# An attention kernel on one core: the order of the 64-query and 192-query pieces in the middle score fill

## The chip, the cores and the metric

The kernel runs on one NeuronCore of a Trainium2 chip. The metric is device time in microseconds (us), the median of the runs that are quoted. The kernel before takes 819.46 us (3 runs, 819.17 to 820.69).

## The reference

```python
B, H, Sq, Sk, D = 16, 32, 192, 1024, 128          # q, k, v are bf16, small random numbers
def reference(q, k, v):
    scale = q.shape[-1] ** -0.5
    scores = jnp.einsum("bhqd,bhkd->bhqk", q, k) * scale
    p = _softmax(scores, axis=-1)
    return jnp.einsum("bhqk,bhkd->bhqd", p, v)
```

There are 512 heads. For each of them the scores are 192 x 1024, softmax runs over the 1024 keys, and the result is 192 x 128.

## The kernel before

The kernel works on **quads** of four heads, 128 of them. Scores are computed transposed, with keys on the partitions: eight tiles of 128 keys times 192 queries give 1536 columns per head. These are made in three **thirds** of 512 columns (one PSUM bank per head). For each third PE (TensorE) runs a **fill** (the score matmuls), ACT (ScalarE) takes the exponential out of PSUM in two instructions, and PE then runs one **PV pass** (32 matmuls) for data of four thirds earlier. So PE's stream is fill, PV, fill, PV, and so on.

In a fill each head has its own 32 rows of the PE array, and the 128-long dot product is done in four passes `w` of 32. Four matmuls, one per head, that differ only in the row group make a **set** below. How a third's 512 columns are cut into pieces is in `CUTS`, as (key tile, first query, last query):

```python
CUTS = (
    (((0, 0, 192),), ((1, 0, 192),), ((2, 0, 128),)),
    (((3, 0, 192), (2, 128, 192)), ((4, 0, 192), (5, 0, 64))),
    (((5, 64, 192),), ((6, 0, 192),), ((7, 0, 192),)),
)
```

The first third has three groups of one piece (12 sets: 192 eight times, 128 four times), the last third the same with the 128 first. The middle third has two groups of two pieces, which alternate: 192, 64, 192, 64, ..., 16 sets. In the code below, shortened and with comments added, a semaphore `s_x` is the one that the trace calls `f_x`.

```python
def take(s, c):
    pe.wait_ge(s, c).then_inc(s, -c)        # wait until s >= c, then take c off it

def qk(f):                                  # fill f: quad x, third b
    x, b = divmod(f, 3)
    if b == 0:
        take(s_qt, 1)
    take(s_kt, 1)
    take(s_e1, 1)
    for group in CUTS[b]:
        for w in range(4):
            h, c = divmod(w, 2)
            for g, (t, n0, n1) in enumerate(group):
                c0 = t * SQ + n0 - 512 * b
                for a in range(4):
                    ...                     # S = the bank of head a, r = its 32 rows
                    ins = pe.matmul(S[:, c0: c0 + n1 - n0],
                                    kt[r, x % NKT, 2 * t + h, :, c],
                                    qt[r, x % R, h, n0:n1, c],
                                    start=w == 0 and g == 0, stop=w == 3, ...)
    ins.then_inc(s_qk, 1)

def pv(s, part=(0, 32)):                    # PV pass s, called after fill s + 4
    x, i = divmod(s, 3)
    if part[0] == 0:
        if i == 0:                          # stands after a MIDDLE fill
            take(s_e3, 3)                   # three exps of the quad are done
            take(s_vp, 2)                   # V is laid out
        if s == NF - 4:
            pe.wait_ge(s_e3, 2)
        elif s < NF - 4 or s == NF - 1:
            take(s_on, 1)                   # the output bank has been read
    ...                                     # 32 matmuls of 129 columns
```

DVE (VectorE) turns each K load and also normalises each PV result, in one order, so a late K holds back a normalisation; PE's next PV pass waits for that one (`f_on` in the trace, `s_on` in the code). And the loads go out on one queue in the order V, K, q, with two additional waits at the start:

```python
for n in range(2, NKN):
    if n == 2:
        e.wait_ge(s_qk, PRE + 1)            # hold V of quad 0
    load_v(n - 2)
    if n == 2:
        e.wait_ge(s_pv, BLANK - 2)          # hold K of quad 2
    load_k(n)
    load_q(e, n)
```

## Time and profile before

| | value | view |
|---|---|---|
| span | 816.9 us | page, head |
| PE busy | 99% | page, part 1 |
| ACT busy | 92% | page, part 1 |
| DMA | 9 tenths or more in 38 of 40 slices, about 405 GB/s | page, part 2 |
| DVE waits for a K load | 15.3 us, 11 times | waits |
| one quad on PE | 2058 + 2107 + 2048 = 6213 ns | matmul starts in the trace |

The head of the page and the rows of part 2 (each digit is the busy share of one fortieth of the span, in tenths):

```profile
span 816.9 us, 71709 instructions
PE 806.7 (99%) x32996; PEld 717.5 (88%) x32996; DVE 599.7 (73%) x1293; ACT 749.8 (92%) x772; POOL 550.7 (67%) x648
...
PE   8999999999999999999999999999999999999997
...
DMA  7999999999999999999999999999999999999992
```

PE and DMA are both full nearly all the time.

The timeline of the kernel before, PE only, for a little over one quad (start us, length us, engine, line, what, count; starts of the next line give the beat, since matmuls overlap):

```profile
397.32 1.10 PE L646 MATMUL f_s<-f_qt,f_kt 32*128 32x192 bf16 x48
398.35 1.10 PE L673 MATMUL f_o<-f_vp,f_pt 128*64 128x129 bf16 x32
399.38 1.10 PE L646 MATMUL f_s<-f_qt,f_kt 32*128 32x192 bf16 x64
400.45 1.10 PE L673 MATMUL f_o<-f_vp,f_pt 128*64 128x129 bf16 x32
401.49 1.09 PE L646 MATMUL f_s<-f_qt,f_kt 32*128 32x128 bf16 x48
402.50 1.10 PE L673 MATMUL f_o<-f_vp,f_pt 128*64 128x129 bf16 x32
403.53 0.35 PE L646 MATMUL f_s<-f_qt,f_kt 32*128 32x192 bf16 x8
```

The fills take 1.03, 1.07 and 1.01 us from their start to the start of their PV pass. The middle one (x64) is the longest although all three stream the same number of columns: that is what the change goes for.

### The profile page before, as it was taken

Reading aid. Unit: us, or ns where it says so; the run is one execution under the profiler, and the core shown is the slowest. Engines: PE = TensorE matmul, PEld = TensorE weight load, DVE = VectorE, ACT = ScalarE, POOL = GpSimd, SP = SyncE. Lnnn points to the kernel's source line nnn. Section 1 sums busy time; section 2 is a strip of 40 time slices with the busy share of each in tenths; the row PEclk is TensorE's granted clock in tenths of the full one; section 3 lists DMA queues with packets and bytes.
Section 4 is the critical chain, followed back from the end, with each engine's and each line's share of the span. In section 5 each row is a group of like instructions: output and inputs, shape, how many; then the busy total and the mean of one; then the engine's idle time right before and its main releaser. Section 6 shows DMA issues by size and latency. Waiting matters only on the chain. (4 is left out here: it accounts for less than half of the span.)

```text
span 816.9 us, 71709 instructions
## 1 busy us (share of the span) xinstructions
PE 806.7 (99%) x32996; PEld 717.5 (88%) x32996; DVE 599.7 (73%) x1293; ACT 749.8 (92%) x772; POOL 550.7 (67%) x648
## 2 busy tenths in 40 slices
PE   8999999999999999999999999999999999999997
PEld 6888888888888888888888888888888888888886
DVE  4777777777777777777777777777777777777775
ACT  6899999999999999999999999999999999999995
POOL 5667766766776676677667666766766676676664
PEclk9999999999999999999999999999999999999999
DMA  7999999999999999999999999999999999999992
GB/s 269 401 402 405 410 403 406 408 403 406 409 401 407 408 403 409 408 402 409 407 403 408 407 403 407 405 405 400 397 406 403 382 411 397 389 404 387 402 368 70
DMA packets 138294, 319.16 MB, mean 391 GB/s; under 512 B 7184, under 2 KB 56336, under 8 KB 121872
## 3 DMA queue, kind: packets, MB, share of 16 engines
q1 hardware_dynamic: 105376, 294.22, 91.9%
q10 hardware_dynamic: 32880, 24.58, 9.0%
q14 instruction: 32, 0.26, 0.1%
q8 instruction: 6, 0.10, 0.0%
HBM read 293.60 MB, written 25.17 MB: 390 GB/s over the span
## 5 line engine op out<-in xcount | busy, mean ns | idle before, releaser
L831 ACT ACTIVATE f_pt<-f_s 128x1536 bf16<-128x1536 f32 x384 | 554.9, 1445 | 0.0
L601 POOL COPY f_kt<-f_kx 128x768 uint32<-128x768 uint32 (+1 forms) x384 | 301.0, 784 | 254.2 <-DVE f_kx L736 254.1
L673 PE MATMUL f_o<-f_vp,f_pt 128*64 128x129 bf16 x12368 | 425.8, 222 | 2.9 <-PEq L629 1.9
L646 PE MATMUL f_s<-f_qt,f_kt 32*128 32x192 bf16 (+1 forms) x20528 | 423.2, 226 | 2.4 <-PEq L629 1.8
L673 PEld LDWEIGHTS f_o<-f_vp,f_pt 128*64 128x64 bf16 x12368 | 366.1, 110 | 55.2 <-issue 28.1
L646 PEld LDWEIGHTS f_s<-f_qt,f_kt 32*128 32x128 bf16 x20528 | 348.5, 92 | 38.9 <-issue 3.1
L736 DVE STREAM_TRANSPOSE f_kx<-f_kn 128x768 uint32<-128x768 uint32 (+1 forms) x384 | 334.0, 870 | 15.7 <-DMA f_kn<-in_k_dram 15.3
L828 ACT ACTIVATE f_pt<-f_s 128x512 bf16<-128x512 f32 x384 | 229.3, 597 | 58.7 <-PE f_s L646 25.6
L610 POOL COPY f_vp<-f_vs 128x1024 uint32<-128x1024 uint32 x256 | 259.9, 1045 | 1.8 <-DMA f_vs<-in_v_dram 1.8
L757 DVE RECIPROCAL f_rinv<-f_o 128x2 f32<-128x2 f32 x381 | 64.9, 170 | 183.2 <-PE f_o L673 183.0
L761 DVE TENSOR_TENSOR f_ob<-f_o,f_rinv 128x256 bf16<-128x256 f32 x381 | 161.7, 424 | 13.3 <-DVE f_rinv L757 0.3
L745 DVE STREAM_TRANSPOSE f_qt<-f_qn 128x384 uint32<-128x384 uint32 x128 | 73.1, 571 | 0.0
L814 ACT ACTIVATE f_pt<-f_ones 128x1536 f32<-128x1536 bf16 x3 | 4.2, 1472 | 0.0
L589 POOL MEMSET f_vp<- 128x1088 uint32 (+1 forms) x3 | 3.8, 1309 | 0.0
L673 PE MATMUL f_s<-f_vp,f_pt 128*64 128x129 bf16 x96 | 3.1, 220 | 0.2 <-PEq L629 0.2
L673 PEld LDWEIGHTS f_s<-f_vp,f_pt 128*64 128x64 bf16 x96 | 2.9, 110 | 0.3 <-issue 0.3
L814 ACT ACT_TABLE_LOAD x1 | 1.3, 1283 | 1.2 <-PEq L859 1.2
L686 PE MATMUL f_o<-f_ones 128*128 128x512 bf16 x2 | 1.0, 622 | 1.1 <-POOL f_ones L586 1.1
L710 DVE MEMSET f_pt<- 128x256 uint32 x4 | 1.1, 272 | 0.9 <-PEq L859 0.9
L703 PE MATMUL f_o<-f_bad,f_ones 128*1 128x1 bf16 x1 | 0.2, 164 | 1.3 <-DVEq L803 1.3
L757 DVE RECIPROCAL f_rinv<-f_s 128x2 f32<-128x2 f32 x3 | 0.5, 170 | 1.2 <-PE f_s L673 1.2
L703 PEld LDWEIGHTS f_o<-f_bad,f_ones 128*1 128x1 bf16 x1 | 0.1, 79 | 1.4 <-DVEq L803 1.4
(15 smaller groups left out, 6.5 us busy)
## 6 DMA issues: line engine op xcount, KB each, us to landing
f_kn<-in_k_dram SPq DMA_DIRECT2D x128, 1024.0 KB, 18.1
f_vs<-in_v_dram SPq DMA_DIRECT2D x128, 1024.0 KB, 16.3
f_qn<-in_q_dram SPq DMA_DIRECT2D x127, 192.0 KB, 14.2
out_dram<-f_ob ACTq DMA_DIRECT2D x62, 384.0 KB, 9.5
out_dram<-f_ob SPq DMA_DIRECT2D x1, 384.0 KB, 3.1
out_dram<-f_ob SPq DMA_DIRECT2D x2, 192.0 KB, 2.0
f_qn<-in_q_dram ACTq DMA_DIRECT2D x1, 192.0 KB, 5.2
```

What stands on the lines that cost most here:

```text
L589: return gp.memset(part.bitcast(U32), 0x3F803F80)
L601: gp.tensor_copy(kt[:, x % NKT].bitcast(U32).rearrange("p U (j s u) c -> p U j s (u c)", s=2, u=2)[:, lo:hi], kx[:, x % 2].rearrange("p (U ...
L610: gp.tensor_copy(vp[:, x % NVP, 2 * T * i: 2 * T * i + 2 * T, 0:D].bitcast(U32), vs[:, x % NVS, 2 * i: 2 * i + 2, :].rearrange("p a (t d) ...
L646: ins = pe.matmul(S[:, c0: c0 + n1 - n0], kt[r, x % NKT, 2 * t + h, :, c], qt[r, x % R, h, n0:n1, c], start=w == 0 and g == 0, stop=w == 3 ...
L673: ins = pe.matmul(O[64 * z: 64 * z + 64, u, 0:129], pt[:, x % R, 2 * y + z, t * SQ + 64 * j: t * SQ + 64 * j + 64], vp[:, x % NVP, (2 * y ...
L736: dve.transpose(kx[:, x % 2].rearrange("p (U s j u) -> p s u U j", s=2, j=32, u=2)[:, :, :, lo:hi], kn[:, x % NKN].rearrange("p (s u U i) ...
L745: dve.transpose(qt[:, x % R].bitcast(U32).rearrange("p b (y j u) c -> p u y b (j c)", y=3, u=2), qn[:, x % NKN].rearrange("p (u y b i) -> ...
L757: dve.reciprocal(ri, O[:, :, 128]).then_inc(s_rc, 1)
L761: dve.tensor_tensor(ob[:, so, 6 * a + 2 * w: 6 * a + 2 * w + 2, :], O[:, :, 0:128], ri.unsqueeze(2).to_broadcast([128, 2, D]), ALU.mult,). ...
L814: return act.activation(part.bitcast(F32), ones[:, 0:1].to_broadcast([128, 2 * T * SQ // 2]), ACT_FN.Copy)
L828: act.activation(pt[:, x % R, 0, c], s1_ps[:], ACT_FN.Exp, scale=scale).then_inc(s_e1, 1)
L831: act.activation(pt[:, x % R, 1:4, c], s3_ps[f % 2][:], ACT_FN.Exp, scale=scale).then_inc(s_e3, 1)
```

## The change: intent and diff

The idea: a fill that ends on a 64-query matmul gives PE little streaming under which to load the weights of the PV pass that follows. With the 64-query piece first, the fill ends on a 192-query matmul. Nothing is added or removed.

```diff
 CUTS = (
     (((0, 0, 192),), ((1, 0, 192),), ((2, 0, 128),)),
-    (((3, 0, 192), (2, 128, 192)), ((4, 0, 192), (5, 0, 64))),
+    (((2, 128, 192), (3, 0, 192)), ((5, 0, 64), (4, 0, 192))),
     (((5, 64, 192),), ((6, 0, 192),), ((7, 0, 192),)),
 )
```

## The prediction

> **What bounds the kernel now.** On the profile page PE is busy 99% of an 816.9 us span: 128 quads (four heads), each three fills and three PV passes. From the last PV matmul before a fill to the last one after it, the trace's matmul starts give medians of 2058 ns (first third), 2107 (middle), 2048 (last): 6.213 us per quad. Between 25 and 801 us no step is over 30 ns off its median, so PE paces that stretch. ACT does not: in the timeline each first exp starts about 50 ns after its fill has ended.
>
> DMA is as close. The page's DMA row reads 9 in nearly every slice, at about 405 GB/s. By packet durations one engine's share of a quad is 8 K packets of 309 ns, 32 V packets of 84, 8 q packets of 65, 16 store packets of 36: about 6.28 us (estimate). The landing records show the 16 engines drifting apart: a K load's first and last arrivals are 1.3 us apart near 55 us, 9 us near 750 us. The last engine decides; its K landings come 6.21 us apart up to quad 76 and 6.26 us after. From K's landing to its use by DVE it is 1 to 2 us in mid-run, 0.02 us by quad 124. DMA has nothing to spare. The Trainium skill, "DMA: Bandwidth & Descriptors" (Latency and other measured facts), says engines 7 and 15 are usually slower; the trace agrees that some lag, but does not number them.
>
> **What the change does.** Nothing is added or removed; only PE's order differs: in the middle fill the sets (four matmuls, one per row group) go 64,192,... instead of 192,64,....
>
> - Close: from the last fill matmul's start to the first PV matmul's it is 160 ns after a 64, 143 after a 128, 172 after a 192. Less streaming (27, 53, 80 ns, estimates from set pitches) 133, 90 and 92 ns are exposed: about 40 ns of PV's weight load is not hidden behind the short matmul. The Trainium skill, "TensorE: Matmul & The Clock Gate" (Part 2), says the next weights load while a matmul runs; these numbers agree.
> - Open: the second set follows the first by 98 ns after 192, 70 after 128: pitch plus 12 to 18 ns. After a 64 I expect 45 to 60 ns, so at most 15 is given back.
>
> Net on PE: middle 2107 -> about 2065 ns (25 to 50 saved), 128 times: 3 to 6.5 us, all on PE's path.
>
> **What remains.** PE would want a quad every 6.17 us; the slowest DMA engine delivers one every 6.21 to 6.26. K's slack is used up earlier, then DVE waits for K, and normalisation and PE behind it. The last K landing (796.15 us) hardly moves; the end can gain about 1 us of slack between DVE and PE. The unprofiled times (819.17 to 820.69; 818.63 profiled) suggest that some runs already wait for DMA.
>
> **Prediction:** 818.9 us, 80% range 816.3 to 820.4. Chances: faster by over 2% 0.005, within 2% 0.985, slower by over 2% 0.01.
>
> **What would show it.** (1) Middle period down 25 to 50 ns, other thirds unchanged. (2) Last fill matmul to first PV matmul in the middle: about 172 ns. (3) In the waits, DVE for the K load grows from 15.3 us to 18 or more, and PE steps well over their median appear from mid-run. (4) Last K landing within 1.5 us of 796.
>
> **What would make it wrong.** If the slow engine speeds up when buffers come free sooner, the whole PE saving shows: 813 to 816 us. If opening on 64 exposes a full weight load (over 40 ns), PE gains nothing.

## The result

| | time, us | runs |
|---|---|---|
| before | 819.32 median (818.6 to 820.69) | 4 |
| changed | 819.79 median (818.35 to 820.86) | 4 |

The ratio is 1.0003, with a 95% interval of 0.9982 to 1.0023: the same. (Ratios here are the mean time of one kernel's fast runs over that of the other's fast runs of the same rounds, so they are not quite the ratio of the medians.) The time lies in the predicted range. The trace, however, does not look as predicted. The head of the changed kernel's page:

```profile
span 817.9 us, 71709 instructions
PE 807.0 (99%) x32996; PEld 718.0 (88%) x32996; DVE 599.3 (73%) x1293; ACT 749.9 (92%) x772; POOL 550.7 (67%) x648
...
DMA  7999999999999999999999999999999999999992
```

PE's timeline of the changed kernel, one quad:

```profile
398.44 1.09 PE L646 MATMUL f_s<-f_qt,f_kt 32*128 32x192 bf16 x48
399.46 1.10 PE L673 MATMUL f_o<-f_vp,f_pt 128*64 128x129 bf16 x32
400.49 1.09 PE L646 MATMUL f_s<-f_qt,f_kt 32*128 32x64 bf16 x64
401.57 1.10 PE L673 MATMUL f_o<-f_vp,f_pt 128*64 128x129 bf16 x32
402.60 1.09 PE L646 MATMUL f_s<-f_qt,f_kt 32*128 32x128 bf16 x48
```

The middle fill begins with 64-column matmuls now, but the PV pass after it still comes 1.08 us after the fill's start (401.57 less 400.49). And in the waits, the line for the K load (us in total, times, longest) reads, before and changed:

```profile
DVE f_kx L736 <- DMA f_kn<-in_k_dram: 15.3, 11, 6.3
DVE f_kx L736 <- DMA f_kn<-in_k_dram: 14.0, 6, 6.9
```

The wait has not grown. So the saving was not made on PE and then hidden by DMA. It was not made on PE at all.

The start times of single records tell where it went. The trace also records PE's semaphore waits: each `take` is a record of the sequencer of 51 ns, whose start is taken here as the moment when it went through (where PE really waits, it comes 37 to 40 ns after the end of what it waits for). For one middle fill of the kernel before, asked by the line of `take`, the view shows three of them:

```profile
L629 PEldq EVENT_SEMAPHORE  x3: 51/51/51, 400.0 to 400.3; - x3
```

Medians over the middle fills, in ns after the start of the last PV matmul before the fill:

| | before | changed |
|---|---|---|
| first matmul of the fill | 153 | 152 |
| second set | 252 | 192 |
| last matmul of the fill | 1069 | 1007 |
| `f_e3` taken | 815 | 816 |
| `f_vp` taken | 971 | 972 |
| `f_on` taken | 1122 | 1123 |
| first PV matmul | 1229 | 1230 |
| last PV matmul (the period) | 2107 | 2107 |

The reordering did what it was meant to: the last matmul of the fill starts 62 ns earlier, and the opening on a 64 gives little back. (The 62 ns are not all gain: in a fill, one set of 192 follows the next after 85 ns and one of 64 after 29, so the last matmul streams some 56 ns longer.) But the first PV matmul starts at the same nanosecond, and so do the three takes ahead of it, one every 150 ns. Each was satisfied well before PE's sequencer came to it: in the kernel before, what they wait for had ended at -871 ns (ACT's exp), 522 ns (POOL's copy of V) and 892 ns (DVE's normalisation). In the other two thirds there is only the take of `f_on`, 40 ns after DVE is done. The sequencer is late because of what it does before: it takes `f_e1` ahead of the fill at -123 ns, 37 ns after ACT's exp has ended, and comes to `f_e3` 939 ns later, with the 64 matmuls of the fill in between (935 ns in the changed kernel). This is read from the traces; no run varies it.

### The profile page after: what moved, and what is told of

Same layout as the page of the kernel before. It is cut to its first block, busy times and chain, and to the rows that moved or that the text cites. A ratio compares the mean times of both kernels' runs of the same rounds, so it can differ in the third digit from the quotient of the medians.

```text
span 817.9 us, 71709 instructions
## 1 busy us (share of the span) xinstructions
PE 807.0 (99%) x32996; PEld 718.0 (88%) x32996; DVE 599.3 (73%) x1293; ACT 749.9 (92%) x772; POOL 550.7 (67%) x648
## 6 DMA issues: line engine op xcount, KB each, us to landing
f_kn<-in_k_dram SPq DMA_DIRECT2D x128, 1024.0 KB, 18.1
```

## The experiments

**Theory T:** the three takes in a row, some 150 ns each on PE's sequencer, hold the PV pass after the middle fill at the same moment in both orders. **Rival W:** the array itself holds it (PV's weight load, a drain), as the prediction had read it. A second question is the prediction's other half: **would DMA have hidden a saving** if there were one?

### e1 and e2: one of the three waits moved ahead of the fill

The exps that `s_e3` counts have ended long before the middle fill starts, and the fill's own wait for `s_e1` implies them (ACT works in order), so the take can stand there without a stall (in e1 `f_e1` is still taken 38 ns after ACT's exp has ended). e1 is this on the changed kernel, e2 on the kernel before.

```diff
 def qk(f):
     ...
     take(s_kt, 1)
+    if b == 1:
+        take(s_e3, 3)
     take(s_e1, 1)
 ...
 def pv(s, part=(0, 32)):
         if i == 0:
-            take(s_e3, 3)
+            if s >= NF - LAG:
+                take(s_e3, 3)
             take(s_vp, 2)
```

> The changed kernel, with PE's wait for the third exp count (f_e3) of the PV pass after the middle fill moved ahead of that fill, between its waits for f_kt and f_e1; it is implied there by f_e1, so it costs no stall. Theory T (three semaphore waits in a row, about 150 ns each on PE's sequencer, hold the first PV matmul after the middle fill at the same moment in both orders): the last of the waits comes about 150 ns earlier, the first PV matmul comes at about 1030 to 1080 ns instead of 1230 after the last PV matmul before the fill, limited by the fill itself; middle period 2107 -> 2050 to 2065 ns early in the run. Rival W (PE is held by something in the array, such as the weight load of PV or a drain): period stays within 10 ns of 2107. For the time: if DMA leaves no room, 818 to 820 us with waits for K by DVE growing; if DMA has room, about 813 us.

> The kernel before with the same move of the wait. Theory T: the middle fill ends on a 64 and the first PV matmul can then follow the last fill matmul by about 115 to 120 ns instead of 160 (streaming 27 plus the 90 that the other fills show); middle period about 2060 to 2070 ns, so the order of the pieces is worth at most about 10 ns once the wait is gone. Rival (the prediction's reading, that 133 ns after a 64 is an exposed weight load): gap stays near 160, period near 2107, and e1 is some 50 ns per middle fill better than e2.

PE's timeline of e1, one quad:

```profile
199.38 1.09 PE L648 MATMUL f_s<-f_qt,f_kt 32*128 32x64 bf16 x64
200.41 1.10 PE L676 MATMUL f_o<-f_vp,f_pt 128*64 128x129 bf16 x32
201.44 1.09 PE L648 MATMUL f_s<-f_qt,f_kt 32*128 32x128 bf16 x48
```

The PV pass now comes 1.03 us after the middle fill's start, not 1.08. In medians, in ns after the last PV matmul before the fill:

| | before | changed | e2 (before + move) | e1 (changed + move) |
|---|---|---|---|---|
| last matmul of the fill | 1069 | 1007 | 1069 | 1007 |
| `f_on` taken | 1122 | 1123 | 970 | 973 |
| first PV matmul | 1229 | 1230 | 1185 | 1177 |
| period of the middle third | 2107 | 2107 | 2063 | 2054 |
| last fill matmul to first PV matmul | 160 | 223 | 116 | 170 |

Theory T holds and W falls. Moving one wait, with no change to any matmul, takes 44 ns off the old order and 53 ns off the new one. It is not the whole 150 ns, since the fill itself then sets the moment; the expectation of e1 had the first PV matmul at 1030 to 1080 ns, too early, but the period in its range. And the gap after a 64 is 116 ns in e2: the old order had no badly hidden weight load either. Take the streaming off (estimated by the pitch of the sets within a fill: medians of 29, 57 and 85 ns for 64, 128 and 192 columns; the prediction's 27, 53 and 80 are a little under them) and 116, 143 and 170 ns leave 87, 86 and 85 ns: what PE needs from a fill to a PV pass is the same whatever the fill ends on. The Trainium skill, "TensorEngine Tiling (Array Packing)" (Tiling Modes, Key Properties), says that a change of tiling mode drains the TensorE, and a fill and a PV pass differ in that (32 rows by 128 columns against 128 rows by 64); the constant 86 ns agrees with it, but no run here takes a drain away, so how much of it is the drain is not shown.

The times hardly moved: e1 818.56 us, ratio 0.998 (0.9959 to 1.0), e2 818.84 us, ratio 0.9987 (0.9967 to 1.0008). 53 ns a quad over 128 quads would be 6.8 us. The waits of e1 say where it went (whole run):

```profile
DVE f_kx L739 <- DMA f_kn<-in_k_dram: 58.9, 80, 7.3
...
PE f_o L676 <- PEq L629: 8.0, 21, 1.1
```

DVE waits for K 80 times, against 6 in the changed kernel, and PE waits at its takes 21 times. From quad 20 on, 100 of 108 K loads are used within 0.05 us of landing (12 before). One such case in e1's timeline (only the lines that matter here):

```profile
684.25 1.09 PE L648 MATMUL f_s<-f_qt,f_kt 32*128 32x64 bf16 x64
...
684.44 0.98 DVE L739 STREAM_TRANSPOSE f_kx<-f_kn 128x768 uint32<-128x768 uint32 x1 [1.50 <-DMA f_kn<-in_k_dram]
685.34 0.13 DVE L760 RECIPROCAL f_rinv<-f_o 128x2 f32<-128x2 f32 x1
...
685.51 0.42 DVE L764 TENSOR_TENSOR f_ob<-f_o,f_rinv 128x256 bf16<-128x256 f32 x1
...
686.05 0.96 PEld L676 LDWEIGHTS f_o<-f_vp,f_pt 128*64 128x64 bf16 x32 [0.88 <-issue]
686.08 1.10 PE L676 MATMUL f_o<-f_vp,f_pt 128*64 128x129 bf16 x32 [0.73 <-PEq L629]
```

DVE stands 1.5 us for K, then turns it, and only then normalises; PE's PV pass, which waits for that normalisation, starts 0.73 us late. After the start, the first such step is at 248 us. The last K lands at 797.21 us, against 796.15 in the kernel before: the end is set by the stream of loads.

### e3 and e4: one more wait, in two places

e3 splits the take of `s_e3` in two where it stands, so that four takes are in a row. e4 is the control: the second half goes ahead of the PV pass after the last fill of a quad. Both are made from the changed kernel.

```diff
 # e3
         if i == 0:
-            take(s_e3, 3)
+            pe.wait_ge(s_e3, 3).then_inc(s_e3, -2)
+            take(s_e3, 1)
             take(s_vp, 2)
 # e4 (and one count more at the start, for the first pass)
+        if i == 1:
+            take(s_e3, 1)
         if i == 0:
-            take(s_e3, 3)
+            pe.wait_ge(s_e3, 3).then_inc(s_e3, -2)
             take(s_vp, 2)
```

> The changed kernel with the f_e3 wait of the PV pass after the middle fill split into two (a wait for 3 that takes 2, then one that takes 1): one more satisfied wait at the same place. Theory T: middle period 2107 -> about 2257 ns, and the time rises by about 128 x 0.15 = 19 us, to about 838 us. Rival W: no change, 819 us.

> Control to e3: the additional wait stands ahead of the PV pass after the last fill of a quad, where there is one wait (f_on), not three. Theory T: there the first PV matmul is held by the fill that is just ending, and a wait of 150 ns more still fits (the one wait is at 775 ns from the fill's start, PV's first weight load at about 1018): last period within 30 ns of 2050, time within 4 us of 819. Rival (any additional semaphore wait costs its 150 ns wherever it stands): about 838 us.

e3: 837.31 us, ratio 1.0209 (1.0182 to 1.0236): slower, though whether by over 2% is unclear. PE's timeline of e3:

```profile
201.66 1.09 PE L646 MATMUL f_s<-f_qt,f_kt 32*128 32x64 bf16 x64
202.89 1.10 PE L674 MATMUL f_o<-f_vp,f_pt 128*64 128x129 bf16 x32
```

The PV pass comes 1.23 us after the fill's start instead of 1.08. The takes stand at 817, 973, 1123 and 1274 ns, the first PV matmul at 1381, and the middle period has a median of 2258 ns, 151 more than before. 128 times 151 ns is 19.3 us; the medians differ by 18.1 us (837.31 less 819.21 of the same rounds).

e4: 820.02 us, ratio 1.0003 (0.9977 to 1.003). The last third's period is 2049 ns, as in the changed kernel (2050). The additional take went through at 582 ns, and the take of `f_on` at 926 ns, as before (927). So a take is free there, though for another reason than the expectation gave: PE's sequencer gets there early and stands at `f_on` until DVE is done at 887 ns, and the additional take fits into that time. In the middle third it comes to the first take at 816 ns only, and each further one is on the path.

The Trainium skill, "Advanced Engine Details and Errata" (Network/Comms), gives 50 to 100 ns for reading a semaphore value from the sequencer. "Perfetto Trace Analysis" (Per-engine timelines, Sequencer-only Instruction) says that only the execution is in the profile, not the semaphore wait or the push and propagation after it. Here the record of a take is 51 ns long, and one more take costs 151 ns: this agrees that the record is not the whole cost, and the measured 151 ns is the number to plan with.

### e5 to e8: the same four kernels with less DMA

Here V is loaded for two of the four heads after the first five quads. The output is wrong; every instruction of PE, DVE, ACT and POOL is kept.

```diff
+    n = 4 if x < NVS else 2
     e.dma_start(
-        vs[:, x % NVS, :, :],
-        vf[4 * x:4 * x + 4].rearrange("a (m t) d -> m a (t d)", t=T),
+        vs[:, x % NVS, 0:n, :],
+        vf[4 * x:4 * x + n].rearrange("a (m t) d -> m a (t d)", t=T),
     ).then_inc(s_v[x % NVS], 16)
```

> The kernel before with half of V's bytes left out after the first five loads (2 of 4 heads are loaded; the output is wrong on purpose), everything else as it was. DMA then has about a fifth less to move. If PE alone paces the kernel before (6.213 us per quad in the profile), the time falls only by the waits at start and end: 815 to 819 us. If DMA already held it for more than that, it falls further.

> The changed kernel with the same lighter V loads. The prediction on record held that DMA hides a saving on PE of 3 to 6.5 us: then this is 3 to 6.5 us faster than e5. Theory T (the three waits hold PV, so PE saves nothing): equal to e5 within 1 us.

> e1 (new order, f_e3 wait moved ahead of the fill) with the lighter V loads. Theory T plus the DMA limit: the saving of 53 ns per middle fill, 6.8 us, now reaches the time: about 7 us below e5, 808 to 812 us, the middle period stays at 2054 ns with no steps far above to the end. If something else than DMA held e1 back, it stays near e5.

> e2 (old order, wait moved) with the lighter V loads. By its middle period (2063 ns) about 5.6 us below e5 and 1 to 1.2 us above e7: that difference is what the order of the pieces is worth by itself. If the order is worth what the prediction said (25 to 50 ns), e7 is 3 to 6 us faster than e8.

| | with all of V, us | with less DMA, us | ratio of the light kernel to the kernel before |
|---|---|---|---|
| before (e5) | 819.17 | 818.94 | 0.9998 (0.998 to 1.0015) |
| changed (e6) | 819.79 | 819.15 | 1.0 (0.9983 to 1.0017) |
| changed + wait moved (e7) | 818.56 | 811.24 | 0.9898 (0.9882 to 0.9915) |
| before + wait moved (e8) | 818.84 | 813.54 | 0.9927 (0.991 to 0.9943) |

(The second column is from other rounds for the last three; the ratio is within the rounds of e5 to e8.) The page of e7 shows the lighter stream, 314 GB/s over the span:

```profile
span 810.8 us, 71709 instructions
...
DMA  7999999999999999999988989999999999999821
...
HBM read 229.11 MB, written 25.17 MB: 314 GB/s over the span
```

Three things follow. First, DMA held neither kernel of the pair (e5, e6 unchanged): the prediction's "PE saves, DMA hides it" did not happen. Note that the DMA row of e7 still reads 8 and 9 with a fifth fewer bytes, so that row alone could never have told. Second, once the wait is moved, DMA does hide the gain: e7 and e8 are 7 and 5 us faster than with all the bytes. Third, the order of the pieces is worth something only then: e7 beats e8 by 2.3 us in the medians. By the periods it should be 14 ns a quad or 1.8 us (2056 + 2054 + 2050 against 2058 + 2063 + 2053), while e8's expectation had 1 to 1.2 us; so the order gives 1.8 to 2.3 us of the 3 to 6.5 us predicted.

### e9 to e12: an earlier start of the DMA stream

If the stream of loads sets the end of e1, starting it earlier should pay. The two waits that hold it back at the start are taken away: both in e9, only the second (K of quad 2) in e10, only the first (V of quad 0) in e12, all on e1; e11 takes both from the kernel before.

```diff
 for n in range(2, NKN):
-    if n == 2:
-        e.wait_ge(s_qk, PRE + 1)
     load_v(n - 2)
-    if n == 2:
-        e.wait_ge(s_pv, BLANK - 2)
     load_k(n)
```

> e1 without the two waits that hold back V of quad 0 (until a count of f_qk) and K of quad 2 (until a count of f_pv) at the start; the loads go out one after the other. In e1 the DMA stream paces the end (K waits with 0.02 us from landing to use), so a stream that starts some 3 to 5 us earlier should end earlier by about as much, 813 to 816 us, if PE's own start is not hurt. If the waits protect the first K and q loads, PE starts later and the gain is lost: 817 to 820 us.

> e1 without the second of these waits only (K of quad 2). About half of the gain of e9 if the stream's early idle time is what counts, with the first loads still protected: 815 to 818 us.

> The kernel before without both waits. There PE paces the stretch from 25 to 801 us, so an earlier DMA stream gives only what PE itself starts earlier, 0 to 2 us: 817 to 820 us, and e9 is at least 2 us faster than it.

> e1 without the first of the two start waits only (V of quad 0 goes out at once, K of quad 2 still waits for the f_pv count). In e9 and e10 the DMA stream had several us in hand, but PE reached its steady beat later, after pauses of 2 to 3.5 us inside a pass (ended by a plain weight load, no semaphore) at 12 to 21 us, when DMA was at full rate. If those pauses come with the loads of quads 2 and up, this keeps e1's start for PE and moves only V of quad 0 earlier by about 2 us: 815 to 818 us. If the stream gains nothing because K of quad 2 sets it, it equals e1: about 818.6 us.

| | time, us | ratio to the kernel before |
|---|---|---|
| e9 | 817.19 | 0.9966 (0.9953 to 0.9979) |
| e10 | 817.37 | 0.9974 (0.9961 to 0.9987) |
| e11 | 823.45 | 1.0043 (1.0029 to 1.0057) |
| e12 | 818.51 | 0.998 (0.9962 to 0.9999) |

In e9 K lies ready for 3.8 us or more in every quad from 20 on (11.0 us at quad 20, 3.8 at quad 100: the loads are slower than PE here too, but start early enough); no PE step between 28 and 799 us is 30 ns over its median. DMA is out of the way, and e9 has the lowest median of the correct kernels, 0.34% below the kernel before (e10 is within its noise). The 813 to 816 us hoped for was missed, as in the second branch of e9's expectation, because PE reaches its steady beat later. K of quad 12 is used at 86.24 us in e9, at 80.95 in e1. PE's timeline of e9 at the start shows why:

```profile
11.75 0.93 PE L672 MATMUL f_o<-f_vp,f_pt 128*64 128x129 bf16 x25
16.22 0.41 PE L672 MATMUL f_o<-f_vp,f_pt 128*64 128x129 bf16 x7 [3.55 <-issue]
16.57 1.72 PE L644 MATMUL f_s<-f_qt,f_kt 32*128 32x128 bf16 x48
...
20.09 1.02 PE L644 MATMUL f_s<-f_qt,f_kt 32*128 32x192 bf16 x38
23.21 0.35 PE L644 MATMUL f_s<-f_qt,f_kt 32*128 32x128 bf16 x10 [2.10 <-issue]
```

PE stops for 3.55 and 2.10 us in the middle of a pass, between plain matmuls, with no semaphore to blame ("issue": nothing that the profile shows). In e1 the same fill pauses for 0.26 us. The granted clock is then 0.5 for 3.4 us at a time, twice (the fill at 16.57 takes 1.72 us instead of 1.09). e11 stops likewise, starts some 6 us later than the kernel before (87.37 against 80.81 us for K of quad 12) and, being held by PE from then on, cannot make it up: 4 us slower, where I had expected 0 to 2 us faster. e12 gave nothing, as the second branch of its expectation said.

What stops PE there can be read from the traces. The page lists a DMA queue of its own for instructions, with six packets of 16384 bytes (e9):

```profile
q8 instruction: 6, 0.10, 0.0%
```

In the first 60 us of the 14 kept traces, 15 times over 350 ns pass from one matmul's start to the next inside a pass. All 15 are ahead of the same two matmuls of PE's stream, the 268th and the 393rd on record, or one matmul earlier in e3 and e4, where one more take has come before. All 15 end 1.23 to 1.48 us after such a packet has landed. Between the two points PE has 125 weight loads, 125 matmuls and 6 takes, 256 instructions. So PE stands for its own instructions, which come by DMA: the packet for the first point starts at 10.68 us in the kernel before and at 13.84 us in e9. The pauses are longest where the loads run at full rate from the start (e9, e10, e11), but e3, with both waits, also had one of 3.85 us (its packet started at 14.7 us). Why a packet starts late is not shown, and no run was made to test this reading.

## Why the prediction was right, and where it was not

The time was right (819.79 us, in the range of 816.3 to 820.4, forecast 818.9), and so was the class. The chain of reasons was mostly not what happened, so the right time was luck.

1. "PE paces that stretch" and "DMA is as close": right. e5 shows that DMA does not hold the kernel before; e1 against e7 shows that DMA holds it as soon as PE is 53 ns a quad faster. The reading of 6.21 to 6.26 us per quad from the slowest DMA engine was the right limit: in e1, which DMA holds, the K landings come 6.20 us apart from quad 20 to 76 and 6.28 after, and the last one was at 797.21 us.
2. "Close: ... about 40 ns of PV's weight load is not hidden behind the short matmul": **the step that failed.** The 160 ns gap after a 64 was longer than streaming plus 86 ns because of three takes at 815, 971 and 1122 ns; with the 192 last, the gap did not become the 172 ns of the prediction but 223. The takes were in the trace of the kernel before, and I had not looked at what stands between the last fill matmul and the first PV matmul on PE's own sequencer. The comparison with the other thirds was not like with like: those have one take.
3. "Open: ... at most 15 is given back": the second set followed after 40 ns instead of 45 to 60. Right in kind, and even cheaper.
4. "Net on PE: ... 25 to 50 saved": zero as the kernel stands (2107 and 2107 ns). With the wait out of the way the order is worth 9 ns per middle third by its period (2063 against 2054).
5. "DVE for the K load grows from 15.3 us to 18 or more, and PE steps well over their median appear": no, 14.0 us and no such steps between 30 and 800 us. Both appeared in e1: 58.9 us, and steps from 248 us on.
6. "Last K landing within 1.5 us of 796": 796.76 us. It held, but because nothing had changed, not because DMA set it.

Two limits stood behind each other, and the prediction named the second one only. Either is enough to make the change worth next to nothing (e1 against e2: 818.56 and 818.84 us with all of V), which is why the time came out right.

## What to carry to other kernels

Before you call a gap between two matmul groups a weight load or a drain, list the semaphore records of PE's sequencer in that gap: a wait that has been satisfied for long still costs about 150 ns of the sequencer, and several in a row add up. Put a wait that is known to be satisfied early where the sequencer has time (here ahead of the fill), and only then judge the order of the matmuls. And when two resources are both full, prove which one holds by making the other lighter: a fifth fewer bytes changed nothing until PE was faster, and then it was worth 7 us.

## What the Trainium skill lacked or had wrong

- "Advanced Engine Details and Errata" (Network/Comms) has 50 to 100 ns for reading a semaphore value. No page has the cost of a wait in PE's stream that also takes the count down: 51 ns in the record, 150 to 156 ns from one to the next, and 151 ns per fill when one was added (e3).
- "TensorEngine Tiling (Array Packing)" says that a change of tiling mode drains the array, without a time. From a 32-row fill to a 64-column PV pass the matmul starts here leave 85 to 87 ns beyond the streaming of the last matmul (estimates), whether that has 64, 128 or 192 columns (e2, e1); how much of this is the drain is not shown.
- "DMA: Bandwidth & Descriptors" (Latency and other measured facts) says that two of the engines are usually slower, and holds the cause that it guesses to be specific to SWDGE (the path through GpSimd); the loads here are on a queue that the profile calls hardware_dynamic. For such loads it has no lag that adds up over a run: in the kernel before, the first and last arrivals of one K load drift from 1.3 us to as much as 9.7 us apart, and in e1 the last one sets what the kernel gets.
- "Runtime: NRT & Kernel Launch" (Instruction fetch mechanics) has no time for the fetch of a block of instructions beside loads that fill the DMA engines: PE stood up to 3.85 us (e3) and went on 1.23 to 1.48 us after the packet had landed (15 pauses).
